# A fused attention and gating block: V computed per 128 tokens and its rows placed by SBUF-to-SBUF loads

## The chip, the cores and the metric

The kernel runs on one core of a Trainium2 chip. The metric is the device time of one execution in microseconds; the median of three runs before the change is 241.07 us (240.92 to 243.4). The core has five engines that work side by side, each with an instruction queue of its own: TensorE (matmuls, in the profile PE, and PEld for its weight loads), VectorE (DVE), ScalarE (ACT), GpSimd (POOL) and SyncE (SP), which here only issues DMA transfers. Sixteen DMA engines carry the transfers. All rows named below refer to the lines of the kernel before the change.

## The reference, cut to what matters

The input x has 2048 tokens of 448 channels, in bfloat16.

```python
# A: 16 heads of 28 channels; each token looks at 8 tokens: itself, 2 back, 4 back, ... 14 back
h  = x + attention(layernorm(x) @ wqkv) @ wo
# B: gated MLP with a 2048 x 2048 mix over the tokens
z  = gelu(layernorm(h) @ w_in)                 # 448 -> 2 x 896
g  = w_sp @ layernorm(z[:, 896:]) + b_sp       # over the tokens
h2 = h + (z[:, :896] * g) @ w_out              # 896 -> 448
```

## The kernel before

**Layout.** The 2048 tokens are two halves of 1024 (index s); unit u (0 to 7) is the 128 tokens at 128u of both halves. After the first layer norm the tokens of a unit are transposed, so that xh holds, for a block c of seven, the channels of the first half's token on partitions 0 to 63 and those of the second half's on 64 to 127. A projection therefore is seven matmuls with 64 rows for each half; the two halves run side by side in the upper and the lower half of TensorE's array.

**q and k** (L757 to L806) are computed for four chunks of tokens, CQ = 0, 512, 768, 896, 1024, the last chunk first. Chunks of up to 256 columns put two groups of heads into one pair of PSUM banks (28 matmuls); the chunk of 512 takes one group at a time (14 matmuls). L783 is the matmul, L797 the eviction (by the helper at L639, so it stands as L641 on ScalarE and L643 on VectorE).

**Attention** (L812 to L931) goes over nine windows i, from 8 down to 0, of 114 tokens plus a halo of 14, in both halves. Since every token looks back by even steps, even and odd tokens of a window (index w) are separate: 64 keys each. For window i:

- V (L819 to L829): 28 matmuls in 64x64 tiles, four tiles side by side: half s by parity w. The lhs is a stride-2 slice of xh, so V comes out with the keys of the window on the partitions, even above odd. Window 0 needs the tail of the first half ahead of the second half's tokens, so xh has a halo of its own (HX = 16 columns), filled by clears on GpSimd (L621) and a copy (L710).

```python
823  iss("pe", lambda e, ...: e.matmul(
824      psum[64 * w:64 * w + 64, bk[s] * 512:bk[s] * 512 + D],
825      xh[64 * s:64 * s + 64, c, HX - HALO + a + w:HX - HALO + a + w + 127:2],
826      wv[64 * s:64 * s + 64, k, :], start=(k == 0), stop=(k == NC7 - 1),
827      tile_position=(64 * s, 64 * w)),
```

- its eviction (L835, 128x896 elements) into one of three rotating V buffers;
- logits (L858, 64 matmuls in 32x64 tiles), exp on ScalarE (L870) into one of two E buffers, the band mask on VectorE (L877), row sums (L886), ln and exp on ScalarE for the reciprocal (L899, L921), the product with V (L911, 64 matmuls in 64x32 tiles) and the scaling on VectorE (L929).

**After attention**, unit by unit: the product with wo (L964), the residual (L972), the second layer norm (L656, L657, GpSimd at L646 and L647, L676), its transpose by DMA (L683, on SP), z2 = second half of w_in (L984), gelu (L994), its layer norm (L1000 to L1014). Between them the first half, z1 (L1028, L1038). Then the token mix g (L1064, 448 matmuls of 512 columns), and the output product (L1093), its add (L1103) and the stores (L1108). g reads w_sp transposed by DMA, 32 transfers of 128x1024 on SP (L946), 16 for the first half of the output tokens (wsp_lo) and 16 for the second, each in its chain waiting for the one before it.

**Weights.** wqkv and w_in come in 448 rows: three blocks of 128 rows and a last one of 64 rows. The last 64 rows are loaded to partitions 0 to 63 (L560, L587). Each projection needs the seven blocks of 64 rows on both halves of the partitions, so small copies cross over: four copies for each of k, q's first and q's second heads (L749 to L753, 64 partitions each), two for v and for each half of w_in (L569, with 3 and 4 blocks).

**The order of the work** is written out: SEQ (L35) lists for each of SP, GpSimd, VectorE, ScalarE and TensorE the numbers of its tasks in the order in which the engine takes them. Semaphore waits are derived from what each task reads and writes (`Sched.issue`, L99). Every engine, SP too, takes its list strictly in order: a transfer that waits holds up all behind it on SP. The cost figures in the planner (L240 to L244) choose only buffers, not the order.

Of the kernel before, what the change touches and what calls it, by code (L numbers as in the profile page):

```python
# [5 lines left out]
S_TOK = 2048  # L6
D = 448
DH = 28
# [13 lines left out]
HX = 16  # L22
XHW = HX + ST + 16
DMA_T = {1: range(5), 2: range(8)}
BLK = ((0, 2, 4, 6, 1, 3, 5), (1, 3, 5, 0, 2, 4, 6))
# [40 lines left out]
)  # L66
NBANKS = 8
NE = 2
NL = 2
NV = 3  # L70
SET_E = "natural_log_exp_and_others"
# [307 lines left out]
def bass_sequential_preLN__sliding_local_dilated__mixer_gmlp__prompt_kernel(  # L379
# [18 lines left out]
    with contextlib.ExitStack() as top:  # L398
# [765 lines left out]
```

## Time and profile before

| | |
|---|---|
| median of the runs (three) | 241.07 us, 240.92 to 243.4 |
| span of the profiled execution, first to last instruction | 241.1 us |
| busy time in it: PE, DVE, ACT, POOL | 234.0, 141.3, 92.9, 27.1 us |
| granted TensorE clock | 1.000 |
| share of the chain that ended last: PE, DVE, POOL | 85%, 5%, 3% |
| DMA packets | 54628, 20.01 MB |
| last store issued on SP | 239.1 us |

The profiled execution gives a span; no other time of that execution is listed, and the median of the runs is the figure beside it. The profile's page is read from the top: busy time of each engine, then the chain of work that ended last, then the groups of instructions by line. A group's line gives busy time, mean duration, the idle time just before its instructions, and what ended that. In the timeline a row is start, duration, engine, line. A duration of TensorE includes the tail of the pipeline, so the start of the next group tells better than the end of one how long a group took; the chain's rows do that.

### The profile page before, as it was taken

To read this page: it belongs to the slowest core of one execution; us is meant where nothing else is said; L and a number is where in the kernel's file an instruction comes from. 1 tells how busy PE (TensorE), PEld (TensorE's weight loads), DVE (VectorE), ACT (ScalarE), POOL (GpSimd) and SP (SyncE) were. 2 spreads that over 40 slices of the span, in tenths; PEclk is the share of its full clock that TensorE was granted. 3 is DMA by queue.
4 is the path that set the end of the run, shared out by engine and by line. 5 is a ranking of instruction groups with operands and counts; after the bars stand their busy time and mean duration, and the time that the engine had idled before them with its cause. 6 is when DMAs were issued, how large, how long until landed. Compare 5 with 4: busy or idle time off the path is not lost.

```text
span 241.1 us, 6691 instructions
## 1 busy us (share of the span) xinstructions
PE 234.0 (97%) x3009; PEld 119.8 (50%) x3019; DVE 141.3 (59%) x280; ACT 92.9 (39%) x111; POOL 27.1 (11%) x68
## 2 busy tenths in 40 slices
PE   7898999999999999999999999999999999999995
PEld 2476865455554444454444444444444444444453
DVE  4998954999999999778820050253101436554443
ACT  2898879859899648665630000000000000000000
POOL 6044000002014023105700000000000000000000
PEclk9999999999999999999999999999999999999999
DMA  7927787732303567998535433200000000010122
GB/s 210 331 57 84 117 136 151 140 78 61 44 4 72 108 112 172 181 161 132 113 83 152 90 87 79 52 3 0 0 0 3 0 0 19 19 61 0 38 93 79
DMA packets 54628, 20.01 MB, mean 83 GB/s; under 512 B 46792, under 2 KB 54472, under 8 KB 54600
## 3 DMA queue, kind: packets, MB, share of 16 engines
q1 hardware_dynamic: 53416, 18.61, 37.9%
q10 hardware_dynamic: 1184, 0.98, 1.4%
q8 instruction: 23, 0.38, 0.7%
q14 instruction: 5, 0.04, 0.0%
HBM read 6.37 MB, written 1.84 MB: 34 GB/s over the span
## 4 chain that ended last, share of the span: by engine, by line
PE 85%; DVE 5%; POOL 3%; issue 2%; DMA 2%; ACT 1%; POOLq 1%; ACTq 0%
PE psum L1064 40%; PE psum L783 9%; PE psum L1093 9%; PE psum L984 8%; PE psum L823 5%; PE psum L964 5%; PE psum L1028 4%; PE psum L858 2%; DMA z2p<-in_A_wqkv_dram 2%; POOL rs L647 2%; PE psum L911 1%; DVE x_tm L972 1%; DVE w_in L643 1%; DVE reg L643 1%; PE psum L886 1%
## 5 line engine op out<-in xcount | busy, mean ns | idle before, releaser
L1073 DVE TENSOR_TENSOR ub<-psum,reg 128x512 bf16<-128x512 f32 x28 | 18.9, 688 | 68.4 <-PE psum L1064 66.0
L1064 PE MATMUL psum<-reg,z2p 128*128 128x512 bf16 x220 | 49.4, 379 | 0.2
L1064 PE MATMUL psum<-wspT_lo,z2p 128*128 128x512 bf16 x218 | 48.5, 379 | 0.4 <-DVE z2p L1014 0.2
L1064 PEld LDWEIGHTS psum<-wspT_lo,z2p 128*128 128x128 bf16 x224 | 21.8, 98 | 26.6 <-issue 0.4
L1064 PEld LDWEIGHTS psum<-reg,z2p 128*128 128x128 bf16 x224 | 21.9, 98 | 26.2
L783 PE MATMUL psum<-xh,reg 64*128 64x128 bf16 (+2 forms) x448 | 26.4, 270 | 0.4 <-issue 0.4
L984 PE MATMUL psum<-w_in,xh 64*128 64x448 bf16 x224 | 22.4, 349 | 0.0
L1093 PE MATMUL psum<-reg 128*128 128x448 bf16 (+2 forms) x119 | 22.2, 342 | 0.1
L1028 PE MATMUL psum<-xh,w_in 64*128 64x512 bf16 x196 | 22.0, 376 | 0.0
L656 DVE BATCH_NORM_STATS2 st<-x_tm 128x6 f32<-128x448 bf16 x32 | 19.5, 610 | 3.6 <-DMA x_tm<-in_A_x_dram 3.5
L783 PEld LDWEIGHTS psum<-xh,reg 64*128 64x128 bf16 x448 | 16.8, 94 | 7.9 <-issue 1.4
L641 ACT ACTIVATE reg<-psum 128x896 bf16<-128x896 f32 (+2 forms) x24 | 19.4, 838 | 1.1 <-PE psum L783 0.9
L1000 DVE BATCH_NORM_STATS2 st<-z2p 128x6 f32<-128x448 bf16 x32 | 17.8, 610 | 1.9 <-ACT z2p L994 1.8
L870 ACT ACTIVATE reg<-psum 128x928 bf16<-128x928 f32 x18 | 16.3, 944 | 5.2 <-PE psum L858 5.2
L994 ACT ACTIVATE z2p<-psum 128x896 bf16<-128x896 f32 x16 | 14.2, 918 | 7.6 <-PE psum L984 7.6
L1038 ACT ACTIVATE reg<-psum 128x1024 bf16<-128x1024 f32 x14 | 13.6, 1026 | 8.4 <-PE psum L1028 8.4
L1093 PEld LDWEIGHTS psum<-reg 128*128 128x128 bf16 x119 | 11.4, 98 | 10.4
L646 POOL TENSOR_SCALAR rs<-mv 128x2 f32<-128x2 f32 x19 | 6.5, 342 | 88.9 <-DVE mv L657 72.3
L1103 DVE TENSOR_TENSOR tring<-psum,x_tm 128x448 bf16<-128x448 f32 (+2 forms) x17 | 10.1, 597 | 10.2 <-PE psum L1093 10.0
L984 PEld LDWEIGHTS psum<-w_in,xh 64*128 64x128 bf16 x224 | 10.6, 94 | 10.5 <-issue 0.4
L1028 PEld LDWEIGHTS psum<-xh,w_in 64*128 64x128 bf16 x196 | 9.4, 94 | 11.5 <-ACT reg L1038 0.2
L647 POOL TENSOR_TENSOR rs<-rs,nhalf 128x2 f32<-128x2 f32 x19 | 14.3, 754 | 1.6
(62 smaller groups left out, 202.7 us busy)
## 6 DMA issues: line engine op xcount, KB each, us to landing
x_tm<-in_A_x_dram SPq DMA_DIRECT2D x15, 112.0 KB, 4.9
out_dram<-tring SPq DMA_DIRECT2D x15, 112.0 KB, 1.7
w_in<-in_B_w_in_dram SPq DMA_DIRECT2D x2, 448.0 KB, 4.7
reg<-in_B_w_out_dram SPq DMA_DIRECT2D x1, 784.0 KB, 6.0
z2p<-in_A_wqkv_dram ACTq DMA_DIRECT2D x2, 336.0 KB, 5.5
reg<-in_B_b_sp_dram SPq DMA_DIRECT2D x1, 512.0 KB, 4.6
w_in<-in_B_w_in_dram SPq DMA_DIRECT2D x2, 224.0 KB, 4.7
reg<-in_A_wo_dram SPq DMA_DIRECT2D x4, 98.0 KB
```

Source lines behind the costliest of these rows:

```text
L641: iss("act", lambda e: e.activation(dst, src, AF.Copy), reads=rd, writes=wr)
L647: iss("pool", lambda e: e.tensor_tensor(dst, dst, nh, ALU.pow), reads=rr + [r_nhalf], writes=rr)
L656: iss("dve", lambda e: e.bn_stats(st[:, b, :], x_tm[:, b, :]), reads=[r_x[b]], writes=[rl[b]])
L783: iss("pe", lambda e, c=c, s=s, gi=gi, lhs=lhs: e.matmul(psum[:, bk[s] * 512 + cw * gi:bk[s] * 512 + cw * gi + cw], lhs, xh[64 * s:64 * s ...
L870: iss("act", lambda e: e.activation(E[:, es[0], 2 * n:2 * n + 2, :], pair_view(lb, 0, 8 * JW), AF.Exp, scale=SCALE), reads=[r_bank[lb[0]], ...
L984: iss("pe", lambda e, k2=k2, c=BLK[s][k2], s=s: e.matmul(psum[:, zb[s] * 512:zb[s] * 512 + D], xh[64 * s:64 * s + 64, c, HX + 128 * u:HX + ...
L994: iss("act", lambda e: e.activation(z2p[:, u:u + 9:8, D * k:D * k + D], pair_view(zb, 0, D), AF.Gelu_apprx_tanh), reads=[r_bank[zb[0]], r_ ...
L1000: iss("dve", lambda e, b=b: e.bn_stats(st3[:, b, k, :], z2p[:, b, D * k:D * k + D]), reads=[r_z2[b][k]], writes=[r_st3[b][k]])
L1028: iss("pe", lambda e, k=k, c=BLK[s][k], s=s: e.matmul(psum[:, bk[s] * 512:bk[s] * 512 + 512], w_in[64 * s:64 * s + 64, k, 128 * f:128 * f ...
L1064: iss("pe", lambda e, b=b: e.matmul(psum[:, gb[0] * 512:gb[0] * 512 + 512], z2p[:, b, 128 * f:128 * f + 128], src[:, b, 512 * (tc % 2):512 ...
L1073: iss("dve", lambda e: e.tensor_tensor(ub[:, us_[0], :], psum[:, gb[0] * 512:gb[0] * 512 + 512], bb[:, 512 * tc:512 * tc + 512], ALU.add), ...
L1093: iss("pe", lambda e, f=f: e.matmul(psum[:, wb[0] * 512 + d0:wb[0] * 512 + d1], z1p[f][:, 128 * m:128 * m + 128], w_out[:, f, d0:d1], star ...
```

## The change

1. **V per unit.** V is computed once for each of the eight units, for both halves, with 14 matmuls in 64x128 tiles (two side by side), tokens in their natural order on the partitions. It is evicted to a staging buffer Vs[u] (8 of them). From there 34 DMA transfers on SP place the rows for each window: for window i, parity w and each unit that the window touches, one transfer takes every second partition of Vs[u] to consecutive partitions of V[i]. Each moves 2 KB for each of its rows. The rows of the transfers are, by window: 8: 63, 63; 7: 56, 8, 56, 8; 6: 49, 15, 49, 15; 5: 42, 22, twice; 4: 35, 29, twice; 3: 28, 36, twice; 2: 21, 43, twice; 1: 14, 50, twice; 0: 57, 7, twice. Every window has a V buffer of its own, in the space that z2 takes later; windows 8 and 0 are cleared first by GpSimd. The gelu writes of z2 wait for the windows and staging buffers that lie in their space. xh loses its halo, and with it the clears of L621 and L622 and the copy of L710.
2. **Three E buffers** in place of two.
3. **q and k end in two pieces**: CQ becomes 0, 256, 512, 768, 896, 1024.
4. **Last weight rows as two loads of 64 partitions.** The last 64 rows of wqkv's and w_in's blocks are loaded to partitions 0 to 63 and again to 64 to 127 (for w_in both halves of the columns in one transfer). The crossing copies become three in place of four for k and q (one of 128 partitions and 4 blocks, two of 64 partitions and 3 blocks) and 3 blocks in place of 3 and 4 for v and w_in.
5. **SEQ is written anew** for all five engines, and some of the planner's cost figures change. In it, k's weights are loaded first (on SP, behind two blocks of x), q's later; k of the last chunks is the first projection, V of units 7 and 6 follows; the copies of the first half of w_in (cpw0) go from VectorE to ScalarE; five instead of seven wsp_lo transposes stand before the first transpose of the second norm; and TensorE's last group is the 304-column piece of the last output block, not the 144-column piece.

```diff
-HX = 16
-XHW = HX + ST + 16
+XHW = ST
-BLK = ((0, 2, 4, 6, 1, 3, 5), (1, 3, 5, 0, 2, 4, 6))
+BLK = ((0, 2, 4, 6, 1, 3, 5), (1, 3, 5, 6, 0, 2, 4))
...
-NE = 2
+NE = 3
-NV = 3
...
         def w_view(dst, src):
-            return ((dst[:, 0:3, :], src[0:384].rearrange("(m p) n -> p m n", p=128), 335.0),
-                    (dst[0:64, 3, :], src[384:448], 154.0))
+            return ((dst[:, 0:3, :], src[0:384].rearrange("(m p) n -> p m n", p=128), 235.0),
+                    (dst[0:64, 3, :], src[384:448], 150.0), (dst[64:128, 3, :], src[384:448], 150.0))
...
-            for h, lo, nb in ((0, 4, 3), (1, 3, 4)):
+            for h in range(2):
...
-                    copy(tk[0].eng, w[64 * h:64 * h + 64, lo:NC7, :], w[64 - 64 * h:128 - 64 * h, 0:nb, :], rs[:-2], [rs[h - 2]])
+                    copy(tk[0].eng, w[64 * h:64 * h + 64, 4:NC7, :], w[64 - 64 * h:128 - 64 * h, 0:3, :], rs[:-2], [rs[h - 2]])
...
+        def ld_winl():
+            for h in range(2):
+                t_winl.append(dma("sp", "winl%d" % h, lambda e, h=h: e.dma_start(w_in[64 * h:64 * h + 64, 3, :], B_w_in[384:448, :]),
+                                  64 * FH * 4, writes=[r_winl[h]], bw=200.0))
...
-                for n, (h, q) in enumerate(((0, 0), (0, 1), (1, 0), (1, 1))):
+                for n, (h0, h1, lo, q) in enumerate(((0, 128, 0, 0), (0, 64, 4, 64), (64, 128, 4, 0))):
...
-        CQ = [0, 512, 768, 896, ST]
+        CQ = [0, 256, 512, 768, 896, ST]
...
+        for u in range(NU - 1, -1, -1):
...
+                for k in range(NC7):
+                    for s in range(2):
+                        iss("pe", lambda e, k=k, c=BLK[s][k], s=s: e.matmul(
+                            psum[:, bk[s] * 512:bk[s] * 512 + D], xh[64 * s:64 * s + 64, c, 128 * u:128 * u + 128],
+                            wv[64 * s:64 * s + 64, k, :], start=(k == 0), stop=(k == NC7 - 1)),
+                            reads=r_w["v"] + [r_xh[u]], writes=[r_bank[bk[s]]])
...
+        def mv(i, u, w, k0, k1, p0, extra, sl=slice(0, 2), sd=slice(0, 2)):
+            n = n_V[i]
+            n_V[i] += 1
+            t_V[i].append(dma("sp", "dV%d_%d" % (i, n), lambda e: e.dma_start(
+                V[i][64 * w + k0:64 * w + k1, sd], Vs[u][p0:p0 + 2 * (k1 - k0) - 1:2, sl]),
+                (k1 - k0) * 2048, deps=[t_evv[u]] + extra, reads=[r_Vs[u]], writes=[r_V[i][n]], issue=0.75, bw=150.0,
+                after=stg_old if i in (1, 2, 3) else ()))
...
+            for w in range(2):
+                for u in units(a - HALO, a + TQ):
+                    k0 = max(0, (128 * u - (a - HALO) - w + 1) // 2)
+                    k1 = min(64, (128 * u + 128 - (a - HALO) - w + 1) // 2)
+                    mv(i, u, w, k0, k1, a - HALO + w + 2 * k0 - 128 * u, extra)
+                if i == 0:
+                    mv(0, NU - 1, w, 0, HALO // 2, 128 - HALO + w, extra, slice(0, 1), slice(1, 2))
```

More of the change, by code (lines that the diff above doesn't have):

```diff
@@ L35 @@
 SEQ = (
[30 rows of a table removed]
[33 rows of a table added]
 )
 NBANKS = 8
-NE = 2
+SPLIT = "q"
+NE = 3
 NL = 2
-NV = 3
 SET_E = "natural_log_exp_and_others"
@@ L482, in bass_sequential_preLN__sliding_local_dilated__mixer_gmlp__prompt_kernel @@
         r_L = [Res("L%d" % i) for i in range(NL)]
-        r_V = [Res("V%d" % i) for i in range(NV)]
+        r_Vs = [Res("Vs%d" % u) for u in range(NU)]
+        r_V = [[Res("V%d_%d" % (i, n)) for n in range(4)] for i in range(NT)]
         r_z1 = [[Res("z1_%d_%d" % (f, t)) for t in range(4)] for f in range(FC7)]
@@ L528, in dve4x, with dma @@
             return (190.0 + 0.26 * n) / 1000.0
-        def dma(eng, name, fn, nbytes, deps=(), reads=(), writes=(), rel=(), store=False, issue=0.62, bw=335.0, after=(), setup=1.0, both=False):
+        def dma(eng, name, fn, nbytes, deps=(), reads=(), writes=(), rel=(), store=False, issue=0.48, bw=335.0, after=(), setup=1.0, both=False):
             def em():
@@ new lines, in bass_sequential_preLN__sliding_local_dilated__mixer_gmlp__prompt_kernel @@
+        cps = t_cp["k", 0] + t_cp["k", 1] + t_cp["q", 0] + t_cp["q", 1]
+        t_V = [[] for _ in range(NT)]
+        n_V = [0] * NT
+        def mv(i, u, w, k0, k1, p0, extra, sl=slice(0, 2), sd=slice(0, 2)):
[5 more added lines that the diff above has]
+                after=stg_old if i in (1, 2, 3) else ()))
@@ L812, in bass_sequential_preLN__sliding_local_dilated__mixer_gmlp__prompt_kernel @@
         t_ot = [None] * NT
+        t_mo = [None] * NT
         for i in range(NT - 1, -1, -1):
             a = TQ * i
-            us = units(a - HALO, a + TQ)
-            vs, bk = [], []
-            rx = [r_xh[b] for b in us] + (r_xpad if i == 0 else []) + ([r_xend] if i == NT - 1 else [])
-            def em(a=a, bk=bk, rx=rx):
-                for k in range(NC7):
-                    for w in range(2):
-                        for s in range(2):
-                            iss("pe", lambda e, k=k, c=BLK[s][k], s=s, w=w: e.matmul(
-                                psum[64 * w:64 * w + 64, bk[s] * 512:bk[s] * 512 + D],
-                                xh[64 * s:64 * s + 64, c, HX - HALO + a + w:HX - HALO + a + w + 127:2],
-                                wv[64 * s:64 * s + 64, k, :], start=(k == 0), stop=(k == NC7 - 1),
-                                tile_position=(64 * s, 64 * w)),
-                                reads=r_w["v"] + rx, writes=[r_bank[bk[s]]])
@@ L975, in bass_sequential_preLN__sliding_local_dilated__mixer_gmlp__prompt_kernel @@
             t_h[u] = th
-            t_hT[u] = ln_unit(u, 2, [th, th], [t_xpad] if u == NU - 1 else [])
+            t_hT[u] = ln_unit(u, 2, [th, th], ())
             tb3 = []
+            lo = [b * FH for b in (u, u + 8)]
+            hit = [i for i in range(1, NT) if any(v_off[i] < o + FH and o < v_off[i] + 1024 for o in lo)]
+            old = [r for i in hit for r in r_V[i]]
+            od = [t_mo[i] for i in hit]
+            for n in range(5):
+                if any(8 * D + 1024 * n < o + FH and o < 8 * D + 1024 * n + 1024 for o in lo):
+                    old.append(r_Vs[n])
+                    od += [t for i in range(NT) for t in t_V[i] if n in units(TQ * i - HALO, TQ * i + TQ)]
             for k in range(2):
```

133 lines of the change are left out of this document (73 added, 60 removed), and 63 rows, old and new, of the table SEQ.

## The prediction

> **What bounds the kernel now.** I read the page first, then the chain of work that ended last, then busy time by stage, then the groups with their shapes kept apart.
>
> ```profile
> PE 234.0 (97%) x3009; PEld 119.8 (50%) x3019; DVE 141.3 (59%) x280; ACT 92.9 (39%) x111; POOL 27.1 (11%) x68
> PE 85%; DVE 5%; POOL 3%; issue 2%; DMA 2%; ACT 1%; POOLq 1%; ACTq 0%
> ```
>
> TensorE is busy for 234.0 of 241.1 us, and the chain of waits runs through it for 85%. By stage (microseconds of the stretch, then busy time with the count of instructions, then clock, DMA share and GB/s):
>
> ```profile
> 20.00:35.00 15.00, 14.29 (x476) 10.59 (x474) 12.48 (x25) 11.61 (x18) 1.32 (x6) 1.00 0.77 110
> 35.00:50.00 15.00, 15.00 (x321) 7.17 (x318) 9.82 (x10) 13.43 (x16) 0.00 (x0) 1.00 0.74 151
> 50.00:70.00 20.00, 19.82 (x663) 11.36 (x662) 19.20 (x29) 16.20 (x19) 2.63 (x4) 1.00 0.24 41
> 70.00:90.00 20.00, 19.81 (x400) 10.27 (x397) 19.10 (x36) 14.58 (x15) 4.82 (x8) 1.00 0.47 87
> 90.00:120.00 30.00, 30.00 (x298) 14.11 (x296) 25.07 (x67) 19.33 (x21) 10.25 (x20) 1.00 0.82 150
> ```
>
> The reader is to see two things. TensorE stands still almost nowhere, so any matmul time taken away shortens the kernel unless a new wait appears. And from 50 to 90 us VectorE is as full as TensorE (38.3 of 40 us), so it is the next limit. The clock is 1.00 throughout; it decides nothing. The chain in order of time shows the only gaps after the start, and the pitch of the matmuls concerned (start, duration):
>
> ```profile
> 9.24 0.56 PE psum L692 x7
> ...
> 9.86 0.96 PE psum L783 x28
> ...
> 16.74 0.37 issue
> ...
> 20.61 0.71 issue
> ...
> 22.03 1.45 PE psum L823 x28
> ...
> 31.20 2.77 PE psum L823 x56
> ...
> 87.69 1.32 PE psum L984 x14
> ...
> 238.61 0.31 DVE tring L1103
> ```
>
> So the kernel's time is: start up to 9.86 us, then TensorE work, then the last add and store. The profiled span, 241.1 us, stands level with the median of the runs, 241.07, so a change of the span can be put on the median as it is. One per cent, 2.4 us, is about what a measurement of this kernel can tell from no change.
>
> **The change, part by part.**
>
> ```profile
> L823 PE MATMUL psum<-reg,xh 64*64 64x448 bf16 x252 | 13.3, 352 | 0.2 <-DVE x_tm L972 0.2
> L783 PE MATMUL psum<-xh,reg 64*128 64x512 bf16 x112 | 13.0, 377 | 0.0
> L783 PE MATMUL psum<-xh,reg 64*128 64x256 bf16 x112 | 6.6, 270 | 0.0
> ```
>
> *V matmuls.* Before, nine windows of 28 matmuls in 64x64 tiles; the chain gives 1.45 us for one alone and 2.77 us for two in a row. Two pairs and five alone make 5.54 + 7.25 = 12.8 us. After, eight units of 14 matmuls with 448 columns in 64x128 tiles, the form of L984: 1.32 us each, 10.6 us, and 0.065 more for each of the two units that stand alone between other tile shapes (1.45 against 2.77/2 = 1.385), 10.7 us. **-2.1 us.** Bounds: -1.8 (all eight with that surcharge) to -2.4 (half of what the busy times, 13.3 less 10.6, would give beyond it).
>
> *q, k end in two pieces.* Eight groups of 14 matmuls with 512 columns (13.0 us busy) become eight groups of 28 with 256 (6.6 us for four, 13.2 for eight). **+0.2 us**; bounds 0 to +0.4. The 1024-column evictions stay the same number.
>
> *Tile shapes.* In the written order TensorE changes tile shape 50 times before and 44 times after; at 0.065 us for a change and the change back, six fewer are 0.2 us, which the V term already holds for the most part. **0**; bounds 0 to -0.2.
>
> *Start.* The first matmul now needs all of k's weights, loaded on SP behind two x blocks, in place of q's on the ACT queue.
>
> ```profile
> 3.13 0.63 DVE L656 BATCH_NORM_STATS2 st<-x_tm 128x6 f32<-128x448 bf16 x1 [3.13 <-DMA x_tm<-in_A_x_dram]
> ...
> 5.78 0.63 DVE L656 BATCH_NORM_STATS2 st<-x_tm 128x6 f32<-128x448 bf16 x1 [0.35 <-DMA x_tm<-in_A_x_dram]
> ...
> 6.63 0.76 ACT L641 ACTIVATE reg<-z2p 64x672 bf16<-64x672 bf16 x1 [0.63 <-DMA z2p<-in_A_wqkv_dram]
> ...
> 7.97 0.40 DVE L676 TENSOR_SCALAR tring<-x_tm,mv,rs 128x448 bf16<-128x448 bf16 x1 [0.25 <-ACT rs L669]
> ...
> 9.10 0.62 DVE L643 COPY xh<-psum 128x896 bf16<-128x896 bf16 x1
> ```
> ```profile
> L641 ACT ACTIVATE reg<-z2p 64x1344 bf16<-64x1344 bf16 x1 | 1.3, 1322 | 0.0
> L643 DVE COPY reg<-z2p 64x1792 bf16<-64x1792 bf16 x2 | 1.2, 603 | 0.0
> ```
>
> The two later x blocks are now second on two queues, not second and third on one, so the 0.35 us wait goes: statistics end near 6.3 instead of 6.62. The weights, as before, near 6.6. On ScalarE two copies of 64x1344 follow, 6.6 + 2 x 1.32 = 9.25; on VectorE one copy of 0.60, then the normalisations and the copy to xh, ending near 9.1. The first matmul at 9.35 instead of 9.86: **-0.5 us**; bounds -0.9 to +0.7 (weights 1.2 us later, by the spread of their landings, less 0.5):
>
> ```profile
> DMA to landing us min/median/max: 4.8/5.6/6.0
> ```
>
> *Idle of TensorE.* 1.08 us of "issue" stand in the chain at 16.74 and 20.61. After, the first V pair and the q blocks are ordered anew, three evictions wait on a ScalarE that does the two long copies, and I find one wait for a PSUM pair of about 0.4 us before the first q block and one of 0.3 before the units 4 and 5. **-0.3 us**; bounds -1.0 to +1.5.
>
> *End.* The last add has 304 columns (0.475 us) instead of 144, 0.31 us. **+0.2 us.**
>
> ```profile
> L1103 DVE TENSOR_TENSOR tring<-psum,x_tm 128x304 bf16<-128x304 f32 x1 | 0.5, 475 | 0.3 <-PE psum L1093 0.3
> ```
>
> *The V loads.* 34 transfers from SBUF to SBUF, 2.3 MB, in rows of 2 KB, four per window (two for window 8), each waiting on SP for the eviction of its unit. No such transfer stands in the trace. Nearest rows:
>
> ```profile
> out_dram<-tring SPq DMA_DIRECT2D x15, 112.0 KB, 1.7
> x_tm<-in_A_x_dram SPq DMA_DIRECT2D x15, 112.0 KB, 4.9
> L553 SPq DMA_DIRECT2D x_tm<-in_A_x_dram x15: 339/432/580, 0.8 to 11.0; - x15
> GB/s 0 29 270 272 337 344 208 308 357 376 385 361 237 86 33 0 0 0 22 124 60 140 39 110 97 70 103 101 160 171 120 129 6 125 225 215 30 154 166 271
> 43.36 14.44 SPq L946 DMA_TRANSPOSE wspT_lo<-in_B_w_sp_dram  x4
> 61.13 0.38 DVE L676 TENSOR_SCALAR tring<-x_tm,mv,rs 128x448 bf16<-128x448 bf16 x1
> 61.54 1.25 SPq L683 DMA_TRANSPOSE xh<-tring  x1
> 69.75 0.73 PE L911 MATMUL psum<-reg 64*32 64x58 bf16 x64
> ```
>
> From below a piece lands 1.7 us after its issue (the store on empty queues), from above 4.9 (x on full ones). The engines have room: 0.24 of their time is used from 50 to 70 us, and 2.3 MB at half of the best rate, 385 GB/s, are 12 us. SP issues 34 x 0.43 to 0.58 us = 15 to 20 us more, in a stage where it has time: four transposes in the 14.4 us from 43.36. The tightest piece is the last of window 2: it stands on SP behind the transpose of unit 7's second norm, which waits for VectorE (61.13 + 0.38, issued 61.54 before; about 60 after), one load of w_in and four more pieces: 60 + 1.25 + 6 x 0.5 = 64.3, landing at 66.0. Its matmuls start at 69.75 before, 2 us less after: 67.7. I take the row of the store, as the engines are near empty there: **0**, cover 1.7 us; bounds 0 to +5.3 (below, second rival).
>
> *Edits off the path, at nothing.* The V evictions (nine of 128x896 become eight), the clears on POOL and two instead of three rows of small copies of k and q lie on engines that TensorE does not wait for. The third E buffer frees a wait that no row shows. Two w_in copies, now 64x2688, go from VectorE to ScalarE: twice 2.6 us by the row of 64x1344, on an engine that idles 5.4 us of 70 to 90 and 10.7 of 90 to 120. Behind them on ScalarE stand gelus that free PSUM, and z1's matmuls wait for the copies; TensorE has 9 us of other work written ahead of z1. If that cover is gone, up to 2.6 us. The last weight rows are loaded twice, 57 KB more each for q, k, v: 0.15 us apiece at 385 GB/s, inside the bounds of the start. The last wsp_lo blocks stand one transpose later on SP, and the first g matmuls ask for them in smaller pieces.
>
> The Trainium skill, "DMA: Bandwidth & Descriptors", section "Rules for kernel authors", advises against two transfers to disjoint partition halves, since both go over the same engines. By it the second load buys nothing in transfer; the copies that it saves are what I counted. No run shows it so far.
>
> **Sum:** -2.1 + 0.2 - 0.5 - 0.3 + 0.2 = -2.5; 241.1 - 2.5 = **238.6 us**. Its own range, from the bounds without all of them at one end, is 237.0 to 240.0.
>
> **The rivals.**
>
> *VectorE becomes the bound.*
>
> ```profile
> L972 DVE TENSOR_TENSOR x_tm<-psum,x_tm 128x896 bf16<-128x896 f32 x8 | 8.6, 1079 | 0.4 <-PE psum L964 0.3
> L643 DVE COPY w_in<-w_in 64x2688 bf16<-64x2688 bf16 x2 | 2.2, 1086 | 0.0
> ```
>
> For it: 38.3 of 40 us busy from 50 to 90, and the masks, adds and norms there stay. Against: TensorE stands still only 0.2 us in each of the two stages, and one w_in copy (1.09 us) leaves the stage, while nothing larger than a V eviction (1.08 us, as L972 on the same size) can enter. If it holds, TensorE's 2.1 us are given back as waits before 90 us, and only part of the start remains: 240.6 us.
>
> *V pieces land late, slower than before.* The place is the attention from 60 to 72 us. Row counts differ: 43 rows twice for window 2, 57 for window 0, 29 twice for window 4. If a piece with an odd count is carried by one of the sixteen engines, 43 rows of 2 KB, 88 KB, at 385/16 = 24 GB/s take 3.7 us. The first such piece holds up the transpose of unit 7 and window 3's last piece behind it on the same engine, the second comes 3.7 us later than counted above. Twice 3.7 less the cover of 1.7 is 5.7, and some 0.4 of it overlaps with TensorE work that stands before those matmuls: 5.3 us, 238.6 + 5.3 = 243.9 us. From a stall of 2.5 us on it decides the sign. For it: nothing in the trace moves odd row counts. Against: the same emptiness of the queues, and that window 2 can be anywhere within 2 us of my estimate.
>
> The Trainium skill states such a rule in "DMA: Bandwidth & Descriptors", section on why a DMA increments its semaphore by 16: the transfer uses the largest number of engines up to 16 that divides both sides' slowest dimension, so 43 or 29 rows run on one engine, 57 on three. By this rule the second rival is the case; by the row of the store (128 rows) the forecast is. The trace of before holds no odd count, so it decides nothing.
>
> *The start comes late.* k's weights arrive at 7.8 instead of 6.6 because x and three large weight loads share the engines; everything shifts by 1.2 us: 239.8 us. For it: landings of 4.9 us. Against: only four x blocks, 448 KB, are issued before them.
>
> **How the numbers follow.** Forecast 0.57, of which 0.40 falls below 238.7 and 0.17 above. Late pieces 0.25: 0.21 above 243.5, 0.04 within one per cent. VectorE 0.10 and start 0.08, both within one per cent. Faster by over 1%: 0.40; within 1%: 0.17 + 0.04 + 0.10 + 0.08 = 0.39; slower: 0.21. Range for 8 in 10: 236.8 (the forecast with the good ends) to 244.2 (the late pieces).
>
> **What would show it.** Right: 112 V matmuls in 10.7 us; first matmul of L783's kind at 9.35; PE idle after that under 1.5 us; V transfers landing in about 2 us; g starting near 118. Wrong: a TensorE wait put down to a DMA into z2p or reg between 40 and 75 us, landings of V pieces that grow with an odd row count, a VectorE wait over 1 us between 50 and 90, or a first matmul after 10.2.

## The result, and the profile after

The changed kernel takes 253.51 us (median of four runs, 252.69 to 254.07) against 241.02 for the kernel before in the same comparison: a ratio of 1.0497, 95% interval 1.0446 to 1.0547. It is 12.5 us slower where the prediction expected 2.5 us less, and outside its range. Medians here are over all executions of a kernel; the ratios leave out the few that ran in a slower state of the chip. The profiled execution took 254.07 us, its span is 252.2 us at a mean granted clock of 0.985.

The page of the kernel after: busy times, clock by fortieths of the span, the queue of instruction packets, and the shares of the chain that ended last.

```profile
PE 234.6 (93%) x2991; PEld 124.7 (49%) x2991; DVE 138.9 (55%) x277; ACT 93.2 (37%) x103; POOL 34.3 (14%) x79
PEclk9999999999996899999999999999999999999999
...
q8 instruction: 23, 0.38, 0.6%
...
PE 83%; DVE 5%; issue 5%; DMA 4%; POOL 1%; ACT 1%; SPq 1%; DVEq 0%; POOLq 0%
```

TensorE is no busier than before (234.6 us against 234.0), but that is now 93% of the span, and the clock dips in two fortieths. "DMA" and "issue" together have risen from 4% to 9% of the chain. Where the time went is seen from one start: g, the token mix. First the kernel before, then the kernel after, both from the timeline of TensorE (start, duration, what ran, in brackets the gap ahead of it and what ended it).

```profile
120.73 45.70 PE L1064 MATMUL psum<-wspT_lo,z2p 128*128 128x512 bf16 x207 [0.16 <-DVE z2p L1014]
```
```profile
10.10 3.30 PE L792 MATMUL psum<-xh,reg 64*128 64x128 bf16 x112
...
30.67 0.39 PE L918 MATMUL psum<-reg,ones 64*32 64x464 bf16 x8 [0.29 <-DVE reg L654]
...
36.82 0.55 PE L890 MATMUL psum<-reg 32*64 32x58 bf16 x45 [1.42 <-issue]
...
43.99 0.54 PE L943 MATMUL psum<-reg,z2p 64*32 64x58 bf16 x48 [0.22 <-DMA z2p<-reg]
...
53.54 0.31 PE L943 MATMUL psum<-reg,z2p 64*32 64x58 bf16 x13 [1.40 <-issue]
...
57.47 0.67 PE L943 MATMUL psum<-reg,z2p 64*32 64x58 bf16 x64 [0.90 <-ACT reg L902]
...
61.01 1.92 PE L792 MATMUL psum<-xh,reg 64*128 64x256 bf16 x32 [1.45 <-issue]
...
71.24 0.35 PE L998 MATMUL psum<-reg 128*128 128x448 bf16 x1 [1.31 <-issue]
...
78.93 0.53 PE L890 MATMUL psum<-reg 32*64 32x58 bf16 x25 [4.36 <-issue]
...
80.51 2.79 PE L1026 MATMUL psum<-w_in,xh 64*128 64x448 bf16 x14
83.23 3.71 PE L998 MATMUL psum<-reg 128*128 128x448 bf16 x16
...
131.38 39.55 PE L1106 MATMUL psum<-wspT_lo,z2p 128*128 128x512 bf16 x182
```

g starts 10.65 us later (131.38 against 120.73); from there to the end the two take 120.8 and 120.4 us. So the loss stands ahead of g, in the stretch of the attention. (That it is 10.65 us and not the 12.5 us of the medians is for the most part the profiled execution of before, a long one; see "The base" below.) Look at the counts in the rows with "issue": 45 of 64 logits, 13 of 64 products, 32 of 56 projections, 1 of 8, 25 of 64. TensorE stops in the middle of a group that has begun, and nothing in the profile is named as what it waited for. The five such gaps are 9.94 us. With the three that name a releaser (0.90, 0.29 and 0.22) it is 11.35 us of gaps after the first projection, where the timeline of before has 1.42: 0.37 and 0.71 of "issue", 0.18 ahead of a V group and 0.16 ahead of g.

The places of these stops tell more. From the stop that ends at 61.01 us to the one that ends at 71.24 TensorE takes 255 matmuls, 255 weight loads and 2 semaphore instructions, together 512 = 2 x 256. From there to 78.93 it is 126, 126 and 4, together 256, and from 36.82 to 61.01 it is 635, 635 and 10, together 1,280 = 5 x 256. Only the stop that ends at 53.54 is off this grid. So four of the five stops stand where a block of 256 instructions ends: what TensorE lacks there is its next instructions. The two "issue" gaps of before, at 16.74 and 20.61, stand 257 instructions apart, one block to within one.

The second loss follows from the longest gap. The stages, then the stretches of 2 us around it (busy time, clock, DMA share, GB/s):

```profile
50.00:70.00 20.00, 16.17 (x511) 10.24 (x506) 15.05 (x22) 14.52 (x17) 3.21 (x4) 1.00 0.75 85
70.00:90.00 20.00, 14.40 (x357) 7.71 (x358) 12.60 (x21) 12.63 (x14) 2.05 (x5) 0.83 0.70 110
```
```profile
74.00:76.00 2.00, 0.57 (x13) 1.00 2.16 82
76.00:78.00 2.00, 0.00 (x0) 0.87 0.07 22
78.00:80.00 2.00, 1.07 (x60) 0.50 0.73 147
...
84.00:86.00 2.00, 2.00 (x11) 0.92 0.75 194
```

After a gap of 4.36 us the granted clock is 0.50 for some 6 us: the 14 matmuls of z2 at 80.51 take 2.72 us to the next start in place of 1.32, and the 16 of L998 after them 3.65. That is some 1.8 us more. Together: gaps +9.9 (11.35 against 1.42), clock +1.8, first projection +0.2 (10.10 against 9.86), V matmuls -1.7 (below). The sum is 10.2 of the 10.65 us that g shows; the rest lies in small differences of the other groups.

What do the DMA engines do while TensorE stands? The view of transfers of the kernel after from 68 to 80 us, in slices of 0.3 us:

```profile
GB/s 120 180 172 65 27 27 20 27 15 99 333 346 209 271 106 55 116 27 14 14 55 7 106 137 205 28 14 14 20 20 20 27 20 27 23 119 292 82 197 253
```

From 75.5 to 78.5 us they move 14 to 28 GB/s, and TensorE starts again at 78.93. A rate of about 25 GB/s is what the second rival gave one engine of sixteen (24). Other transfers are held meanwhile: the 383 packets that start between 75 and 76 us, most of them not of the V piece, take 409.6% of sixteen engines' microsecond, 66 us in all. The V pieces themselves, two of their four kinds, by their line on SP (count, min/median/max of the issue, first and last start):

```profile
L849 SPq DMA_DIRECT2D z2p<-z2p x18: 621/747/3565, 31.0 to 72.2; - x18
...
L849 SPq DMA_DIRECT2D reg<-z2p x2: 687/706/725, 63.9 to 74.6; - x2
...
DMA to landing us min/median/max: 3.0/3.1/3.2
```

An issue costs about 0.75 us, not 0.43 to 0.58. A landing is recorded only for the two pieces of 15 rows, 3.0 to 3.2 us after their issue, so whether landings grow with odd row counts, one of the prediction's signs, can't be read here.

### The profile page after: what moved, and what is told of

It reads as the page before. It is cut to its first block, busy times and chain, and to the rows that moved or that the text cites. A ratio compares the mean times of both kernels' runs of the same rounds, so it can differ in the third digit from the quotient of the medians.

```text
span 252.2 us, 6714 instructions
## 1 busy us (share of the span) xinstructions
PE 234.6 (93%) x2991; PEld 124.7 (49%) x2991; DVE 138.9 (55%) x277; ACT 93.2 (37%) x103; POOL 34.3 (14%) x79
## 4 chain that ended last, share of the span: by engine, by line
PE 83%; DVE 5%; issue 5%; DMA 4%; POOL 1%; ACT 1%; SPq 1%; DVEq 0%; POOLq 0%
PE psum L1106 38%; PE psum L1026 9%; PE psum L1135 8%; PE psum L1070 8%; PE psum L998 5%; PE psum L792 5%; PE psum L943 2%; PE psum L890 2%; PE psum L828 2%; DMA z2p<-in_A_wqkv_dram 2%; DMA x_tm<-in_A_x_dram 1%; DVE st L667 1%; DVE tring L687 1%; PE psum L918 1%; DVE reg L909 1%
## 5 line engine op out<-in xcount | busy, mean ns | idle before, releaser
L1106 PE MATMUL psum<-wspT_lo,z2p 128*128 128x512 bf16 x224 | 49.3, 379 | 0.0
L792 PE MATMUL psum<-xh,reg 64*128 64x256 bf16 (+1 forms) x560 | 26.3, 248 | 1.6 <-issue 1.5
L792 PEld LDWEIGHTS psum<-xh,reg 64*128 64x128 bf16 x560 | 22.5, 94 | 4.3 <-issue 1.6
L1026 PE MATMUL psum<-w_in,xh 64*128 64x448 bf16 x224 | 23.7, 363 | 0.0
L657 POOL TENSOR_SCALAR rs<-mv 128x2 f32<-128x2 f32 x22 | 8.3, 376 | 79.8 <-DVE mv L668 61.5
L658 POOL TENSOR_TENSOR rs<-rs,nhalf 128x2 f32<-128x2 f32 x22 | 16.5, 750 | 1.8
L962 DVE TENSOR_TENSOR reg<-psum,reg 128x912 bf16<-128x912 f32 x9 | 11.1, 1235 | 10.0 <-PE psum L943 10.0
L1135 PEld LDWEIGHTS psum<-reg 128*128 128x128 bf16 x119 | 11.4, 98 | 10.2
L652 ACT ACTIVATE reg<-psum 128x1024 bf16<-128x1024 f32 (+2 forms) x17 | 13.9, 852 | 6.3 <-PE psum L792 6.2
```

Of the source, the lines that this page charges most:

```text
L652: iss("act", lambda e: e.activation(dst, src, AF.Copy), reads=rd, writes=wr)
L658: iss("pool", lambda e: e.tensor_tensor(dst, dst, nh, ALU.pow), reads=rr + [r_nhalf], writes=rr)
L792: iss("pe", lambda e, c=c, b=BLK[s][c], s=s, gi=gi, lhs=lhs: e.matmul(psum[:, bk[s] * 512 + cw * gi:bk[s] * 512 + cw * gi + cw], lhs, xh[6 ...
L1026: iss("pe", lambda e, k2=k2, c=BLK[s][k2], s=s: e.matmul(psum[:, zb[s] * 512:zb[s] * 512 + D], xh[64 * s:64 * s + 64, c, 128 * u:128 * u + ...
L1106: iss("pe", lambda e, b=b: e.matmul(psum[:, gb[0] * 512:gb[0] * 512 + 512], z2p[:, b, 128 * f:128 * f + 128], src[:, b, 512 * (tc % 2):512 ...
L1135: iss("pe", lambda e, f=f: e.matmul(psum[:, wb[0] * 512 + d0:wb[0] * 512 + d1], z1p[f][:, 128 * m:128 * m + 128], w_out[:, f, d0:d1], star ...
```

## Experiments

**The theories.** A: the transfers whose row count leaves them one engine (29, 43; 57 leaves three) hold that engine, and what TensorE waits for in mid-group, its own instructions, ends behind them; V pieces behind them come late too. B: any such traffic does it, by its bytes. C: SP is late, at 0.75 us for each of 34 pieces. D: the number of pieces over few engines matters beyond the worst three row counts. The order of the runs follows from these: mend the worst counts, mend all, put single-engine traffic into the kernel before, move the issue to other queues, shrink the pieces, thin them, leave them out. The kernel before took 241.0 to 241.5 us (medians) beside all of them.

**1. The worst row counts in two pieces.**

```diff
-            one transfer of (k1 - k0) rows
+            return {29: [16, 13], 43: [32, 11], 57: [48, 9]}.get(r, [r])
```

> The changed kernel with only the V pieces of 29, 43 and 57 rows sent as two transfers each (16+13, 32+11, 48+9 rows). Theory A (a transfer is carried by as many engines as divide its row count, so 43 or 29 rows go over one engine at about 27 GB/s, and TensorE's instruction loads wait behind them): TensorE's gaps in the middle of a group, 10 us between 35 and 79 us in the changed kernel, fall under 4 us, the 4.4 us gap at 74.6 is gone, g starts near 124 instead of 131.4, time 244 to 247 us. Theory B (the gaps come from 2.3 MB more traffic and 34 more issues as such, or from the denser instruction stream of the new order): gaps and time as in the changed kernel, 253 to 254 us.

Measured: 246.86 us, ratio 1.0212 (1.0149 to 1.0275). The timeline of TensorE of this run:

```profile
55.53 0.67 PE L958 MATMUL psum<-reg,z2p 64*32 64x58 bf16 x64 [1.75 <-ACT reg L946]
...
70.95 0.38 PE L905 MATMUL psum<-reg 32*64 32x58 bf16 x25 [1.09 <-issue]
...
73.22 0.73 PE L958 MATMUL psum<-reg,z2p 64*32 64x58 bf16 x64 [1.57 <-DVE mv L668]
...
125.63 39.33 PE L1121 MATMUL psum<-wspT_lo,z2p 128*128 128x512 bf16 x178 [0.16 <-issue]
```
```profile
74.00:76.00 2.00, 2.00 (x12) 0.50 0.66 149
```

6.6 of the 12.5 us are back by cutting six transfers in two, and the gap of 4.36 us, ahead of the same 25 logits, is 1.09. As A has it. 5.6 us are left. The waits of 1.75 and 1.57 us are now at the start of a product with V. Ahead of the second, the VectorE instruction named had ended at 72.25, 0.97 us before, and the last piece of that window went out on SP from 70.96 to 71.72: it is probably what the product waits for. Ahead of the first, the ScalarE instruction named ended at 55.29, 0.24 us before, and the last piece of that window went out up to 53.64; which of the two it was isn't shown. The clock takes part again: by the second row it is 0.50 after the stops of 1.09 and 1.57 us, which have 0.7 us of work between them. z2 and the product with wo take some 2 us more by their starts than in runs 9 and 10, where the clock stays at 1.00.

**2. Every piece as a multiple of 16 and a rest.**

```diff
+            return [x for x in (r // 16 * 16, r % 16) if x]
```

> The changed kernel with every V piece cut into a multiple of 16 rows and a rest below 16, so that no engine carries more than 4 rows of a transfer; 26 transfers more on SP. Theory A: the remaining gaps (pieces of 49, 50, 35 and 63 rows on 5 to 10 engines) shrink too, time 240 to 244 us, unless SP becomes late: 26 issues of 0.75 us are 20 us of SP. Theory B: more transfers make it worse, 254 us or more.

Measured: 258.38 us, ratio 1.0698 (1.0652 to 1.0744): worse than the change itself. From this run's timelines, TensorE and SP:

```profile
62.88 0.73 PE L958 MATMUL psum<-reg,z2p 64*32 64x58 bf16 x64 [4.46 <-issue]
...
84.47 0.73 PE L958 MATMUL psum<-reg,z2p 64*32 64x58 bf16 x64 [3.59 <-DMA z2p<-z2p]
```
```profile
84.29 1.37 SPq L859 DMA_DIRECT2D reg<-z2p  x2
```

The last V piece is issued at about 85 us, where the kernel after had its last at 74.6. No stop by "issue" is left in the middle of a group, as A has it. In their place stand stops at the head of one: 4.46 us without a name and 3.59 us by name for a piece, both ahead of a whole product with V, and 2.64 us ahead of row sums, for VectorE. The clock is 0.50 from 36 to 38, 64 to 68 and 84 to 88 us, so part of the loss is the clock. That it is the twenty-six more issues on SP that make the pieces late, as C has it and A's own proviso, fits the late issues; it is argued, not tried by itself.

**3, 4, 5. Transfers that nobody waits for, in the kernel before.** Three SBUF-to-SBUF transfers on SP at about 56 us, in rows of 2 KB, with 43, 48 and 57 rows. Nothing of the change is in these kernels.

```diff
+                iss("sp", lambda e, n=n: e.dma_start(z2flat[0:43, 8192 + 1024 * n:9216 + 1024 * n], z2flat[0:43, 0:1024]),
+                    reads=stg_old, writes=[r_dum[n]], prod="dma", inc=16)
```

> The kernel before, with three transfers of 43 rows of 2 KB from SBUF to SBUF (unused space) added on SP behind the seventh wsp_lo transpose, near 58 us; nothing waits for them but the gelus after 80 us. Theory A: one engine is busy for about 10 us from 59 us on; TensorE shows gaps in the middle of groups between 60 and 72 us, together 3 to 8 us, and the transposes of the second norm land late; time 244 to 249 us. Theory B: 264 KB of traffic at a quiet place cost nothing, 241 to 241.5 us.

> As the one before, with 48 rows in each of the three transfers instead of 43: more bytes, but a row count that sixteen engines divide. Theory A: no gap, 241 to 241.5 us. Theory B: the same as with 43 rows.

> The kernel before with three added transfers of 57 rows, which three engines divide (19 rows each, 1.4 us at 27 GB/s, 4.3 us for the three). Theory A: between 48 rows (241.5 us, no gap) and 43 rows (249.7 us, one gap of 6.2 us): a gap of 0 to 2 us and 241.3 to 244 us. If the row count did not set the number of engines, more bytes than with 43 rows would cost more than with 43.

Measured: 43 rows 249.65 us, ratio 1.0337 (1.0253 to 1.0422); 48 rows 241.54, 1.0004 (0.9978 to 1.0031); 57 rows 241.45, 1.0018 (0.9995 to 1.0041). More bytes cost nothing, fewer cost 8 us: B falls as the account of this loss. The run with 43 rows, its timeline, its transfers from 56 to 76 us in slices of 0.5 us, and a stretch of its clock:

```profile
70.14 0.95 PE L823 MATMUL psum<-reg,xh 64*64 64x448 bf16 x5 [6.17 <-issue]
```
```profile
GB/s 166 244 135 1 7 13 25 25 25 57 25 38 96 120 99 26 25 25 25 29 25 25 25 25 25 25 25 69 133 0 0 33 0 0 0 0 0 0 0 0
```
```profile
70.00:72.00 2.00, 1.86 (x73) 0.50 0.18 42
```

264 KB at 25 GB/s are 10.6 us, from 58 to 69.5. TensorE stops after 23 of 28 matmuls and goes on when the stretch has ended; then the clock is 0.50. Counted from TensorE's first instruction, matmuls, weight loads and semaphores, the stop comes after 3,266 = 12 x 256 + 194; the four stops of the kernel after come after a multiple of 256 and 193. It is the end of a block again. With 57 rows no stop stands in the middle of a group, and the transfers from 56 to 76 us show why (slices of 0.5 us):

```profile
GB/s 61 122 111 10 224 104 74 106 82 66 74 99 170 150 69 76 186 0 0 0 0 0 0 0 0 33 0 0 0 158 212 89 33 0 0 0 0 16 0 0
```

The lowest rates of the stretch are 66 to 76 GB/s, three times 25, and it is over at 64.5.

Where its instructions come from can be read from the queue of instruction packets. The page gives 23 of them, 0.38 MB, so 16.5 KB each; with 2,991 matmuls and as many weight loads that is one for some 260 instructions of TensorE. Where they fall, in the run with 43 rows (60 to 61 us, then 62 to 71 and, within it, 63 to 64: packets, MB, share of 16 engines) and in the run with 48 rows (62 to 71 us):

```profile
q8 instruction: 1, 0.02, 7.7%
```
```profile
q1 hardware_dynamic: 996, 0.41, 106.1%
```
```profile
q1 hardware_dynamic: 161, 0.06, 553.6%
```
```profile
q1 hardware_dynamic: 647, 0.16, 9.0%
q8 instruction: 2, 0.03, 1.3%
```

With 48 rows a packet comes about every 4 to 5 us. With 43 rows one comes between 60 and 61, then none from 62 to 71, and the next between 71 and 72, after TensorE has gone on. Other transfers are held: the 161 packets that start between 63 and 64 take 553.6% of sixteen engines' microsecond, 89 us in all; with 48 rows the whole stretch from 62 to 71 stands at 9.0%. The instruction packet itself is short (7.7% of sixteen engines for 1 us is 1.23 us), so by its record it was over by 62; yet TensorE, which stops at 63.97, goes on only when the transfers on one engine end. The kernel after has the same pattern: a packet of that queue at 72.7, none of it from 73 to 81, the stop of 4.36 us up to 78.93. That TensorE lacks instructions is shown by the places of the stops. That the instruction packet lies on the same engine as the transfer, and that it is its completion that waits, is inferred from these times; the trace names neither.

Three rules of the Trainium skill bear on this. "DMA: Bandwidth & Descriptors", section on why a DMA increments its semaphore by 16, has 43 rows on one engine, 48 on sixteen, 57 on three: the three runs agree. The same page, "Queues, rings and completion order", says that a completion is written only after every earlier write from that engine, across its queues: that fits the packet that was read at 60.7 and of use at 70, and no run here proves it. "Runtime: NRT & Kernel Launch", section "Instruction fetch mechanics", has instructions fetched in blocks of 16 KiB, 256 instructions, and calls the cost mostly hidden: the size agrees with 16.5 KB, the cover does not hold here, 6.17 us.

**6. The same 43 rows at another time.** Again the kernel before, with the three transfers at 152 us, in the token mix.

> The kernel before with the three 43-row transfers of 2 KB rows of the earlier run (249.65 us, a stop of 6.17 us), now issued on SP at about 153 us, in the token mix, where TensorE takes 128 matmuls of 512 columns in some 27 us for each instruction packet of the trace (packets at 130, 157, 184 and 211 us in the kernel before). If the stop comes from instruction packets that end behind the transfer on its engine, a hold-up of about 10 us is covered there and the time stays at 241.3 to 242. If the transfers on one engine disturb TensorE in another way (its reads of SBUF, the clock), it loses several us here too, 245 to 250.

Measured: 241.39 us, ratio 1.0006 (0.9983 to 1.0029). Its transfers from 148 to 172 us in slices of 0.6 us, their issue on SP, and the instruction packet between 155 and 156:

```profile
GB/s 12 175 192 58 0 0 73 230 137 24 20 7 17 51 24 27 14 0 0 10 17 14 14 14 24 27 24 3 0 3 14 17 10 10 24 27 24 17 0 0
```
```profile
151.98 13.30 SPq L1124 DMA_DIRECT2D xh<-xh  x3
```
```profile
q8 instruction: 1, 0.02, 5.9%
```

The run isn't quite run 3 at another time. There SP issued the three within 1.94 us and they ran without a break; here each waits for the one before it (issued at 151.98, 158.37 and 164.72), and the rates show three slow stretches of 4 to 5 us with pauses. A single 43-row piece was enough for the stop of 4.36 us in the kernel after. Here a packet falls into the first stretch and TensorE doesn't stop: a packet's instructions last 27 us in the token mix (128 matmuls at 216 ns), in the attention 4 to 5. So one-engine traffic doesn't disturb TensorE wherever it runs; the result fits that it matters where instructions are used up faster than the hold-up lasts. Eleven microseconds in one piece weren't tried here.

**7, 8. V pieces issued on GpSimd's and on ScalarE's queue**, with the worst counts split as in run 1.

```diff
-                    iss("sp", lambda e, at=at, r=r: e.dma_start(
+                    iss("pool", lambda e, at=at, r=r: e.dma_start(
```

> The split of the worst pieces as in the first experiment, with all V pieces issued from GpSimd's queue instead of SP's, at the places where they stood. What is left of the loss (246.9 against 241.3 us) has two explanations. Theory C: SP is late, since a V piece takes 0.75 us of it and the transposes of the second norm and the later pieces stand behind; then the time falls to 240 to 242 us, unless GpSimd's own issue is dear. Theory D: pieces that still go over 5 to 9 engines (63, 49, 50, 35 rows) hold up others; then 246 to 247 us as before.

> The same with all V pieces issued from ScalarE's queue. Theory C: the SP waits go, but ScalarE pays 40 issues of 0.5 to 0.75 us, 20 to 30 us of an engine that is 70 to 80 per cent busy there: 241 to 246 us. Theory D: 246 us or more.

Measured: GpSimd 247.52 us, ratio 1.0212 (1.0148 to 1.0277); ScalarE 245.69, 1.0188 (1.0153 to 1.0224). Run 1 had 1.0212, so neither queue gives a clear gain over SP. On ScalarE the waits for pieces are exchanged for waits for ScalarE itself (timeline of TensorE of that run):

```profile
50.73 1.70 PE L792 MATMUL psum<-xh,reg 64*128 64x256 bf16 x28 [1.87 <-ACT reg L917]
...
71.12 0.28 PE L958 MATMUL psum<-reg,z2p 64*32 64x58 bf16 x11 [1.24 <-issue]
```

The second row is a stop in mid-group, and the run on GpSimd has such stops too (1.99 and 1.19 us in its profiled execution, the longest of its four), so SP's queue alone isn't what makes them. On GpSimd the issue takes 0.53 us and GpSimd is busy for 17.5 of the 40 us from 50 to 90, so that queue has room. With SP freed of all pieces the time on GpSimd's queue is nearer D's 246 to 247 us than C's 240 to 242: what is left in run 1 is not SP's time alone.

**9, 10, 11. Smaller, thinner, fewer pieces.** At most 16 rows each; these with an eighth of their bytes; and one piece of at most 16 full rows for each window, 9 in place of 34. These three kernels leave out the rest of V and clear four of the V buffers instead, so they show time alone; in the last the product also waits for that one piece only. The edit of the first:

```diff
-                V[i][64 * w + k0:64 * w + k1, sd], Vs[u][p0:p0 + 2 * (k1 - k0) - 1:2, sl]),
+                V[i][64 * w + k0:64 * w + min(k1, k0 + 16), sd], Vs[u][p0:p0 + 2 * (min(k1, k0 + 16) - k0) - 1:2, sl]),
```

> The changed kernel with every V piece shortened to its first 16 rows (or to all, where it has fewer), so that part of V is never placed: the 34 issues and waits on SP stay, the bytes fall to a third and no engine carries more than one row of a piece. Theory A alone: no gap in the middle of a group. Theory C: waits of the V product for its pieces remain as in the first experiment, 243 to 246 us. Theory D: they go, 239.5 to 241.5 us.

> The kernel after with each V piece cut to at most 16 rows and, of every row, to 2 of 16 heads in each half (256 B in place of 2 KB), V buffers 4 to 7 cleared; so most of V is never placed. The number of transfers and their issues on SP stay at 34; their bytes fall to about an eighth of those of the 16-row run (244.6 us). If the last 3.3 us over the kernel before (241.3) are bytes on the engines, the time falls to 241 to 242.5. If they are the issues on SP (34 at 0.75 us) or the new order of the work, it stays at 244 to 245.

> The kernel after with one V piece of at most 16 rows for each window, 9 transfers in place of 34; so most of V is never placed. SP issues 25 transfers less, about 19 us of its time. If the issues on SP hold the rest of the loss, the time falls to 241 or below, and by the terms of the forecast alone (V matmuls -1.7, as measured, the rest level) to 239.5. If the new order of the work itself (start, tile shapes, waits) costs them, it stays at 243.5 to 245, and the gaps in the middle of groups are still there.

Measured: 244.61 us, ratio 1.0142 (1.0077 to 1.0206); thin 245.04, 1.0123 (1.0090 to 1.0157); nine pieces 242.47, 1.0032 (0.9999 to 1.0065); the profiled execution of the last, 240.97 us, is the fastest of its ten. The timeline of TensorE, first with 34 thin pieces, then with nine:

```profile
43.31 0.54 PE L948 MATMUL psum<-reg,z2p 64*32 64x58 bf16 x48 [0.65 <-DMA z2p<-reg]
...
80.09 0.54 PE L948 MATMUL psum<-reg 64*32 64x58 bf16 x47 [1.33 <-issue]
...
120.84 39.55 PE L1111 MATMUL psum<-wspT_lo,z2p 128*128 128x512 bf16 x182
```
```profile
66.98 0.38 PE L897 MATMUL psum<-reg 32*64 32x58 bf16 x22 [0.52 <-issue]
...
77.49 0.50 PE L950 MATMUL psum<-reg 64*32 64x58 bf16 x43 [0.41 <-issue]
...
118.21 39.55 PE L1113 MATMUL psum<-wspT_lo,z2p 128*128 128x512 bf16 x182
```

Taking seven eighths of the bytes away changes nothing that these runs can tell; taking 25 of 34 issues away gives 2.6 us, in the medians and at the start of g (120.84 against 118.21); by the ratios it is 2.2. So the number of transfers, with the waits for them, has a price of its own, about 0.1 us each: part is a wait for a piece, part are stops in mid-group that shrink with it. The stops of 1.33 and 0.41 us come after the same number of TensorE's instructions, 15 x 256 + 194, so here too TensorE stands at the end of a block. How many small transfers make the next block late, these runs don't tell.

Neither case of the expectation came true: with nearly all pieces gone the kernel should have been at 241 or below, at 239.5 by the V matmuls alone, or else at 243.5 to 245. It is at 242.5, level with the kernel before or a little behind it.

**12. Three E buffers in the kernel before.**

```diff
-NE = 2
+NE = 3
```

> The kernel before with three E buffers in place of two, nothing else changed. The forecast costed this at nothing since no row shows a wait for an E buffer: 241.0 to 241.6 beside 241.3. If the exp of a window waits for a buffer in a way that the rows hide, it gains 0.5 us or more.

Measured: 241.57 us, ratio 1.0003 (0.9980 to 1.0026). Nothing, as costed. The first projection and g in this run, to set beside 10.10 and 118.21:

```profile
9.46 0.96 PE L783 MATMUL psum<-xh,reg 64*128 64x128 bf16 x28
...
118.64 45.93 PE L1064 MATMUL psum<-wspT_lo,z2p 128*128 128x512 bf16 x212
```

No version tried is faster than the kernel before.

## Why the prediction was wrong, step by step

**The failing step: "The V loads".** It took the row of the store, a transfer of 128 rows, for pieces of 7 to 63 rows, and so cost them at 0 with an upper bound of 5.3. The steps of the loss, by medians: splitting the 29, 43 and 57 row pieces gives back 6.6 us (253.5 to 246.9); cutting all to 16 rows another 2.3 (to 244.6), which is within the spread of the two runs; an eighth of the bytes nothing; leaving out 25 of the 34 another 2.6 (245.0 to 242.5). Together that is some 11 us for a term put at 0.

**The second rival** named the right cause, row counts that leave a transfer one engine, at the right rate (24 GB/s worked out, 25 measured), and its sign; its price, 243.9, was 9.6 us short. It counted a V piece that waits for another, and that wait is small: by name 0.22 us, at most 1.12 with the 0.90 ahead of another product. It didn't count that TensorE's own instructions can come late (8.54 us in the four stops at the ends of blocks, 9.94 in all five), nor the clock after a long stop (1.8 us). The prediction's "The clock is 1.00 throughout; it decides nothing" read a property of a TensorE without gaps as a property of the kernel. The sentence that set rule against row, "By this rule the second rival is the case; by the row of the store (128 rows) the forecast is", was the right question; the row was of a count that the change doesn't use.

**SP's time.** "34 x 0.43 to 0.58 us = 15 to 20 us more": it is 34 x 0.75 = 25.5 us by the median, and more with the long ones (one took 3.57 us). By name it cost the kernel after little; run 2 suggests how near it was to a bound.

**V matmuls, -2.1.** Right in kind, a little large. Groups of the kernel after, shapes kept apart:

```profile
L828 PE MATMUL psum<-reg,xh 64*128 64x448 bf16 x112 | 11.8, 350 | 0.0
L792 PE MATMUL psum<-xh,reg 64*128 64x256 bf16 x336 | 19.7, 269 | 1.5 <-issue 1.5
```

By the starts of what follows, the 112 take 11.1 us, not 10.7, against 12.8 before: -1.7. A unit followed by projections of the same tile shape takes 1.32 to 1.34 us; the four followed by attention or other shapes take 1.41 to 1.53, where the forecast had 1.385 for two of them. The lower bound, "all eight with that surcharge", is 12.8 - 8 x 1.385 = 1.7 us, not 1.8, so the result is at the edge of the bounds.

**q, k in two pieces, +0.2.** Busy time rises by 0.1 (19.7 against 13.0 + 6.6); by starts it is 19.04 against 19.07 us. 0, within its bounds.

**Start, -0.5.** The first projection starts at 10.10, and at 9.7 to 9.9 in runs 9 to 11, against 9.46 to 9.86 for the kernel before. The chain of the kernel after (start, duration):

```profile
2.17 5.42 DMA z2p<-in_A_wqkv_dram
```

k's weights landed at 7.59, not 6.6: near the third rival's 7.8, at a cost of 0.2 to 0.4 us here, so +0.2 to +0.4 for -0.5, inside the bounds. Whether x and the other loads on the engines made them late, as that rival has it, no run tells. What of it is the second load of the last rows, which the Trainium skill advised against ("DMA: Bandwidth & Descriptors", "Rules for kernel authors"), no run tells.

**Idle of TensorE, -0.3.** It can be read from run 11, where the stops are nearly gone, beside run 12, which is the kernel before but for an E buffer without effect. Run 11 starts g 0.43 us earlier (118.21 against 118.64), where the forecast, without its term for the end, had 2.7. By the starts in the two timelines: V -1.7, q and k -0.4, the product with wo -0.2; against that the first projection +0.4, gaps after it +0.8 (1.1 against 0.3), logits +0.4 and z2 +0.3. So what the V matmuls gain, the start and the new order give back, each term small: +0.8 for -0.3 is inside the bounds of that step. The 1.08 us of "issue" from which the forecast started are in the one profiled execution of before; run 12 has 0.31 us of gaps in all. From g on, run 11 takes 120.8 us and run 12 120.7: the end, +0.2, is about right.

**VectorE as the bound.** It isn't: 27.7 of 40 us busy from 50 to 90 in the kernel after, and no wait of TensorE on it over 0.3 us. In run 11, without the long stops, it is 37.2 of 40, and TensorE still doesn't wait for it there. Off-path edits at 0: shown for the E buffer (run 12); the w_in copies and the double weight loads weren't tried alone.

**The base.** "The profiled span, 241.1 us, stands level with the median": the runs since list both, and a time is 1.7 to 2.1 us above its span (239.6 for 241.38). So the profiled execution of before was one of about 243 us, some 2 us off the median that its span was set against. In it g starts at 120.73, in run 12 at 118.64. As a sum of differences the forecast loses little by that.

## What to carry to other kernels

Before moving work to DMA, divide each transfer's row count by 16: a count such as 43 runs at one engine's rate (25 GB/s here; 29 wasn't tried alone), and what it held up here was TensorE's supply of instructions, where matmuls are short. A stop in the middle of a group, with nothing named, is worth counting: instructions between two stops that come to a multiple of 256 point to the supply. Cost each added transfer by its issue on its queue (0.75 us here) and look for who has that time, since splitting bad counts into good ones buys engines with issues. Here a gain of 2 us of matmul was no gain, since it needed 34 transfers to place its result.

## What the runs showed of the hardware

- A transfer of 43 rows of 2 KB moves at 25 GB/s; three of them (264 KB) took about 11 us and cost 8 us, three of 57 rows cost nothing (run 3 against run 5).
- TensorE can stop for over 6 us in the middle of a group, with "issue" as the only name in the profile. Four of five such stops in the kernel after, and the one in run 3, stand at the ends of blocks of 256 of its instructions. No packet of the instruction queue q8 is recorded during the stops of 4.36 and 6.17 us; the same transfers 95 us later, one at a time, where packets are 27 us apart, cost nothing.
- After a stop of 4.36 us the granted clock was 0.50 for some 6 us; after 6.17 us, for at least 8, from within the stop on. Single stops of 1.3 to 1.45 us left it at 1.00, but in run 1 it fell to 0.50 after stops of 1.09 and 1.57 us with 0.7 us of work between them. The Trainium skill, "TensorE: Matmul & The Clock Gate", Part 1, has half rate after an idle window of about 3.4 us; the two long stops agree, run 1 doesn't: no stop there was as long as that.
